# Splitting weights without GpSimd and adding taps in pairs ahead of TensorE, in a dynamic convolution with a gated MLP

## The chip, the cores and the metric

The kernel runs on one core of a Trainium2 chip. The metric is the device time of one launch in microseconds (us). The kernel before was timed three times: 1320.76, 1321.1 and 1321.77 us, median 1321.1 us.

## The reference

Two steps follow each other. For each of 4 x 4096 positions a softmax over 7 taps (8 heads) weighs the position and the six before it; then each of the 16384 rows of 192 goes through a gated MLP of width 1536.

```python
w = softmax(weight_gen)                     # over the last axis, 7 taps, per head
out = einsum('bshk,bskhg->bshg', w, x_unf)  # x_unf: the row and the six rows before it
g, val = out @ w_gate, out @ w_val          # 192 -> 1536, twice
y = (g * sigmoid(g) * val) @ w_out          # 1536 -> 192
```

x and weight_gen are fp32; the three weight matrices arrive as float64, two 32-bit words per number.

## The kernel before, in words

**Groups and steps.** The 16384 rows are 32 groups (g) of 512 rows: 128 partitions by JG = 4. The width of 1536 is 12 blocks (f) of 128. A step (g, f) makes the two products of one block for one group (lines L464 to L487, 18 matmuls of 512 columns), ScalarE's silu (L491), VectorE's product h (L500 for groups 0 and 1, L505 for the others), and, two steps later, the product with w_out (L539 or L550 and L559). PSUM has four banks for `up`, which is two steps: step s+2 can't begin before VectorE has read the sums of step s. An fp32 operand is split into a high part and a low rest (`hi` by a copy on ScalarE, `lo` by a subtraction), and three products are added.

**Order of the steps** (L645 to L649). Steps 0 to 3 are (0, 0) to (0, 3); then (1, f) and (0, f + 4) alternate up to step 19; (1, 8) to (1, 11) are steps 20 to 23, and from step 24 on the groups come one after the other. Nothing reorders instructions: each engine runs them in the order in which this Python emits them. A dictionary `todo` holds, by step, the pieces of other work that are emitted around h of that step. In steps 0 to 3 all pieces come ahead of h, later only the first one.

**Blocks of weights** (`weight_ops`, L387 to L450). Each block of 128 columns becomes fp32 and is split. In the kernel before a block takes five DMAs on SP's queue (L380), the exponent's bits (L394, VectorE), Relu and Sign (L403, L405, ScalarE), sign times scale (L406, GpSimd), the mantissa in two operations (L411, L421, VectorE), the value (L434, VectorE), copies on ScalarE (L384, L448) and two subtractions on GpSimd (L385). Later `wo32` is split too (L384, L385, called at L663).

**The first two groups** (`summed_turn`, L274 to L299). Each of the seven taps is a product x times weight on VectorE (L230), a copy of 64 columns on ScalarE (L286), and eight transposing matmuls against an identity, added up in PSUM (L289). The tile `xatt` has two buffers. From group 2 on VectorE adds the taps itself (L230, L251) and the turn goes by a 32x32 transpose and DMAs (L304 to L342). `split_ops` (L344 to L363) splits the turned sums.

**GpSimd's queue.** TensorE's sum of one step is made by two half-arrays. `told` (L265) puts a nop on GpSimd's queue that waits for the first part of the sum; `behind` makes the first matmul of the second part (L483) wait for that nop. So the nop also waits for all that stands ahead of it on GpSimd's queue.

Of the kernel before, what the change touches and what calls it, by code (L numbers as in the profile page):

```python
# [18 lines left out]
def dynconv_glu_kernel(  # L19
# [23 lines left out]
    nc = tc.nc  # L43
# [41 lines left out]
    ident = const.tile([P, P], F32, name="ident")  # L85
    warm = const.tile([P, 1], F32, name="warm")
    exp_bias = const.tile([P, 1], F32, name="exp_bias")
    wa_hi = const.tile([P, 2, F], F32R, name="wa_hi")
    wa_lo = const.tile([P, 2, F], F32R, name="wa_lo")
    wb_hi = const.tile([P, F], F32R, name="wb_hi")  # L90
    wb_lo = const.tile([P, F], F32R, name="wb_lo")
    wo = const.tile([P, NF, 2, D], F32R, name="wo")
    wo32 = const.tile([P, NF, D], F32, name="wo32")

# [126 lines left out]
    def attention_ops(g):  # L221
        cx, cw = chunk_of(xcuts, g), chunk_of(wcuts, g)
        jx, jw = g * JG - xcuts[cx][0], g * JG - wcuts[cw][0]
        last = K - 1
        tmp = {}

        def mul(engine, k, into):
            src = x_t[cx][:, jx + k : jx + k + JG].rearrange("p t (h i) -> p t h i", h=H)
            w = e_t[cw][:, jw : jw + JG, :, k : k + 1].to_broadcast([P, JG, H, G])
            engine.tensor_tensor(  # L230
                out=into.rearrange("p t (h i) -> p t h i", h=H), in0=src, in1=w, op=ALU.mult
            )

        if g < MOVED:
            return mul

        def first():
            xatt[g] = att.tile([P, JG, 2 * P], F32, tag="xatt", name="xatt")
# [35 lines left out]
    def summed_turn(g):  # L274

        mul = attention_ops(g)
        if g == 0:
            ps = [ps_up.tile([P, NC], F32, tag="up", name="tr") for _ in range(2)]
        else:
            ps = [ps_dn.tile([P, NC], F32, tag=f"dn{2 + n}", name=f"tr{n}") for n in range(2)]  # L280

        def tap(k):
            def go():
                a = att.tile([P, JG, 2 * P], F32, tag="xatt", name="xatt")
                mul(nc.vector, k, a[:, :, 0:D])
                nc.scalar.activation(out=a[:, :, D:], in_=a[:, :, P:D], func=AF.Copy)  # L286
                for half in range(2):
# [16 lines left out]
    def turn_ops(g):  # L304

        whole = {}

        def blocks():
            cut = att.tile([P, JG, D], F32, tag="cut", name="cut", bufs=1)
            cut = whole["cut"] = cut.rearrange("p t d -> p (t d)").rearrange(  # L310
                "p (i t c) -> p i t c", i=NB, t=JG
            )
            nc.vector.transpose(
                cut, xatt[g][:, :, 0:D].rearrange("p t (i r) -> p i t r", i=NB)
            )
# [27 lines left out]

    def split_ops(g, ps):  # L344
# [15 lines left out]

            return go

        return [high(0), low(0), high(1), low(1)] if g < MOVED else [high(1), low(1), high(0), low(0)]  # L363


    NW = 3 * P + D
    raw_t = {}

    def load_weights(f):
        raw = stage.tile([P, NW, 2], I32, tag="raw", name="raw", bufs=RAW)  # L370
        fs = slice(f * P, (f + 1) * P)
        pieces = (
# [4 lines left out]
            (raw[:, 3 * P : NW], w_out[fs]),  # L377
        )
        for dst, src in pieces:
            nc.sync.dma_start(out=dst.rearrange("p n w -> p (n w)"), in_=src.bitcast(I32))  # L380
        raw_t[f] = raw

    def split(hi, lo, src):
        nc.scalar.activation(out=hi, in_=src, func=AF.Copy)  # L384
        nc.gpsimd.tensor_tensor(out=lo, in0=src, in1=hi.bitcast(F32), op=ALU.subtract)  # L385

    def weight_ops(f):  # L387
        st = {}
# [2 lines left out]
        def exponent():  # L391
# [28 lines left out]
        def mantissa_low():  # L420
# [5 lines left out]
                op0=ALU.logical_shift_right,  # L426
                op1=ALU.bitwise_or,
            )
            if f + RAW < NF:
                load_weights(f + RAW)  # L430

        def value32():
            w = stage.tile([P, NW], F32, tag="w", name="w")
            nc.vector.scalar_tensor_tensor(  # L434
                out=w,
                in0=st["m"],
                scalar=float(2**24),
                in1=st["scale"],
                op0=ALU.add,
                op1=ALU.mult,  # L440
            )
            split(wb_hi[:, fs], wb_lo[:, fs], w[:, 2 * P : 3 * P])
            split(
                wa_hi[:, :, fs],
                wa_lo[:, :, fs],
                w[:, 0 : 2 * P].rearrange("p (i n) -> p i n", i=2),
            )
# [164 lines left out]
    with tc.manual_schedule():  # L612
        nc.gpsimd.memset(exp_bias, -920.0 * TWO23)

        nc.scalar.activation(out=warm, in_=exp_bias, func=AF.Exp)
        now, soon = load_x(0)
        for op in load_taps(0) + [now]:
            op()
        load_weights(0)
        load_weights(1)  # L620
        soon()
        for f in range(2, RAW):
# [9 lines left out]
        for op in after[:6]:  # L632
            op()
        ps, taps = summed_turn(0)
        meanwhile = w0 + w1[:2]
        for op in taps[:2] + after[6:]:
            op()
        for op, other in zip(meanwhile, taps[2:] + [lambda: None]):
            op()
            other()  # L640
# [13 lines left out]
        for f in range(2, NF):  # L654
# [31 lines left out]
        for i in range(len(steps) + LAG + 1):  # L686
# [67 lines left out]
```

## Time and profile before

| | |
|---|---|
| median of three runs | 1321.1 us |
| the profiled execution's own time | 1320.99 us |
| its span | 1319.2 us |
| TensorE busy | 1284.0 us (97%) |
| VectorE busy | 1006.8 us (76%) |
| ScalarE busy | 589.6 us (45%) |
| GpSimd busy | 49.9 us (4%) |
| mean granted TensorE clock | 0.990 |
| TensorE's chain L483, L471, L550, L474 | 22%, 22%, 19%, 18% of the span |

A row of a view of groups or of the timeline gives the line of the kernel, the engine, the operation, what is written from what, the shape, and how many; a timeline row begins with the start and the duration in us, and in brackets stands the idle time ahead of it and what ended it. A busy share near 100% on TensorE says that matmuls follow each other, not that the array is at its peak. The whole execution has few idle places; the view by slices shows them in the first two or three of forty slices and in the last.

### The profile page before, as it was taken

Reading aid. Unit: us, or ns where it says so; the run is one execution under the profiler, and the core shown is the slowest. Engines: PE = TensorE matmul, PEld = TensorE weight load, DVE = VectorE, ACT = ScalarE, POOL = GpSimd, SP = SyncE. Lnnn points to the kernel's source line nnn. Section 1 sums busy time; section 2 is a strip of 40 time slices with the busy share of each in tenths; the row PEclk is TensorE's granted clock in tenths of the full one; section 3 lists DMA queues with packets and bytes.
Section 4 is the critical chain, followed back from the end, with each engine's and each line's share of the span. In section 5 each row is a group of like instructions: output and inputs, shape, how many; then the busy total and the mean of one; then the engine's idle time right before and its main releaser. Section 6 shows DMA issues by size and latency. Waiting matters only on the chain.

```text
span 1319.2 us, 31481 instructions
## 1 busy us (share of the span) xinstructions
PE 1284.0 (97%) x13280; PEld 1233.0 (93%) x13280; DVE 1006.8 (76%) x1397; ACT 589.6 (45%) x1039; POOL 49.9 (4%) x59
## 2 busy tenths in 40 slices
PE   6898999999999999999999999999999999999997
PEld 5777888889999999999999999999999999999997
DVE  7368787778887777888777798777778877777843
ACT  4235344454444345444444544444454444444443
POOL 4234000000000000000000000000000000000000
PEclk9899999999999999999999999999999999999999
DMA  6230221211122121122212112221211212111010
GB/s 178 72 124 13 62 83 30 83 42 47 54 57 75 38 83 41 26 71 62 71 42 83 38 27 73 59 71 42 82 29 31 80 31 81 41 42 34 20 42 13
DMA packets 64150, 74.89 MB, mean 57 GB/s; under 512 B 6924, under 2 KB 53516, under 8 KB 62216
## 3 DMA queue, kind: packets, MB, share of 16 engines
q1 hardware_dynamic: 64008, 72.89, 20.1%
q8 instruction: 103, 1.69, 0.5%
q14 instruction: 39, 0.32, 0.1%
HBM read 48.48 MB, written 24.38 MB: 55 GB/s over the span
## 4 chain that ended last, share of the span: by engine, by line
PE 89%; DVE 5%; ACT 3%; issue 2%; DMA 1%; POOL 0%; SPq 0%; ACTq 0%; DVEq 0%; POOLq 0%
PE up L483 22%; PE up L471 22%; PE dn L550 19%; PE up L474 18%; PE dn L559 3%; PE tr L289 2%; PE dn L539 1%; DVE h L505 1%; DVE prod L230 1%; ACT sg L491 1%; DVE lo L508 0%; DVE xatt L230 0%; ACT L491 0%; ACT L183 0%; DVE m L421 0%
## 5 line engine op out<-in xcount | busy, mean ns | idle before, releaser
L550 PE MATMUL dn<-wo,hi 64*128 64x384 f32 x2880 | 553.9, 344 | 0.4 <-ACT hi L506 0.4
L559 PE MATMUL dn<-wo,lo 64*128 64x192 f32 x2880 | 487.8, 249 | 0.3 <-DVE lo L508 0.3
L550 PEld LDWEIGHTS dn<-wo,hi 64*128 64x128 f32 x2880 | 449.2, 184 | 11.0 <-ACT osb L588 1.4
L559 PEld LDWEIGHTS dn<-wo,lo 64*128 64x128 f32 x2880 | 428.6, 186 | 4.5 <-DVE lo L508 0.5
L506 ACT ACTIVATE hi<-h 128x512 fp32r<-128x512 f32 x360 | 228.3, 634 | 359.1 <-DVE h L505 359.1
L505 DVE TENSOR_TENSOR h<-up,sg 128x512 f32<-128x512 f32 x360 | 248.0, 689 | 179.4 <-ACT sg L491 179.2
L491 ACT ACTIVATE sg<-up 128x512 f32<-128x512 f32 x384 | 228.9, 596 | 339.3 <-PE up L483 330.4
L508 DVE TENSOR_TENSOR lo<-h,hi 128x512 fp32r<-128x512 f32 x360 | 246.6, 685 | 80.4 <-ACT hi L506 80.4
L483 PE MATMUL up<-xhi,wa_hi 64*128 64x512 f32 x768 | 214.7, 421 | 8.3 <-POOLq L267 8.1
L471 PE MATMUL up<-xhi,wb_hi 64*128 64x512 f32 x768 | 216.0, 421 | 5.0 <-ACT xhi L349 4.1
L471 PE MATMUL up<-xlo,wb_hi 64*128 64x512 f32 x768 | 203.9, 392 | 1.6 <-DVE xlo L356 1.5
L471 PE MATMUL up<-xhi,wb_lo 64*128 64x512 f32 x768 | 204.7, 394 | 0.0
L474 PE MATMUL up<-xhi,wa_hi 64*128 64x512 f32 x768 | 203.4, 391 | 0.0
L474 PE MATMUL up<-xhi,wa_lo 64*128 64x512 f32 x768 | 203.4, 391 | 0.0
L483 PE MATMUL up<-xhi,wa_lo 64*128 64x512 f32 x768 | 202.8, 390 | 0.0
L474 PE MATMUL up<-xlo,wa_hi 64*128 64x512 f32 x768 | 202.4, 388 | 0.0
L483 PE MATMUL up<-xlo,wa_hi 64*128 64x512 f32 x768 | 202.0, 388 | 0.0
L251 DVE TENSOR_TENSOR xatt<-xatt,prod 128x768 f32<-128x768 f32 x180 | 172.5, 958 | 0.0
L230 DVE TENSOR_TENSOR prod<-xt,wt 128x768 f32<-128x768 f32 x180 | 171.5, 953 | 0.2
L483 PEld LDWEIGHTS up<-xhi,wa_hi 64*128 64x128 f32 x768 | 121.8, 185 | 11.7 <-POOLq L267 11.6
L471 PEld LDWEIGHTS up<-xhi,wb_hi 64*128 64x128 f32 x768 | 121.7, 184 | 7.6 <-ACT xhi L349 4.6
L474 PEld LDWEIGHTS up<-xhi,wa_hi 64*128 64x128 f32 x768 | 122.0, 185 | 5.6
(56 smaller groups left out, 1326.8 us busy)
## 6 DMA issues: line engine op xcount, KB each, us to landing
xt<-in_x_dram SPq DMA_DIRECT2D x14, 1344.0 KB, 6.9
turned<-cut SPq DMA_DIRECT2D x120, 96.0 KB, 2.0
out_dram<-osb SPq DMA_DIRECT2D x116, 96.0 KB, 1.9
t<-turned SPq DMA_DIRECT2D x60, 128.0 KB, 2.6
t<-turned SPq DMA_DIRECT2D x30, 256.0 KB, 2.9
raw<-in_moe_w_out_dram SPq DMA_DIRECT2D x12, 192.0 KB, 2.7
wt<-in_weight_gen_dram SPq DMA_DIRECT2D x3, 672.0 KB, 5.6
raw<-in_moe_w_gate_dram SPq DMA_DIRECT2D x12, 128.0 KB, 2.3
```

The costliest lines, as they stand in the source:

```text
L230: engine.tensor_tensor(out=into.rearrange("p t (h i) -> p t h i", h=H), in0=src, in1=w, op=ALU.mult)
L251: nc.vector.tensor_tensor(out=a, in0=a, in1=tmp.pop(k), op=ALU.add)
L289: nc.tensor.matmul(ps[half][:, t * P : (t + 1) * P], a[:, t, half * P : (half + 1) * P], ident, start=(k == 0 and t == 0), stop=(k == K - ...
L471: nc.tensor.matmul(ps, w[r, fs], m[r], start=(n == 0), stop=False)
L474: ins = nc.tensor.matmul(sums[i], w[r, i, fs], m[r], start=False, stop=False)
L483: ins = nc.tensor.matmul(sums[i], w[r, i, fs], m[r], start=False, stop=(n == len(full) - 1))
L491: nc.scalar.activation(out=sg, in_=sums[0], func=AF.Silu)
L505: nc.vector.tensor_tensor(out=h, in0=sums[1], in1=sg, op=ALU.mult)
L506: nc.scalar.activation(out=hi, in_=h, func=AF.Copy)
L508: nc.vector.tensor_tensor(out=lo, in0=h, in1=hi.bitcast(F32), op=ALU.subtract)
L550: nc.tensor.matmul(acc[g, t], hi[r, cs], wo[r, f].rearrange("p a d -> p (a d)"), start=opens, stop=False,)
L559: nc.tensor.matmul(acc[g, t][:, 0:D], lo[r, cs], wo[r, f, 0], start=False, stop=closes)
```

## The change

- `SUMS`: group 0's taps go to TensorE as five tiles (0), (1), (2), (3+4), (5+6), group 1's as four, (0+1), (2+3), (4+5), (6). VectorE makes the products and adds a pair; `xatt` has three buffers. A turn starts with its upper half, which needs ScalarE's copy.
- In group 1 the products of tile n stand in the order before step n (those of tile 0 before step 0), and its turn behind the matmuls of step n.
- No work but nops and memsets is left on GpSimd: the sign is put into the scale's bits by one VectorE operation (`value32`), the Sign on ScalarE is gone, and the rests of a block are one subtraction on VectorE (`low32`, 128x384). The high parts of a block are one copy on ScalarE. The rest of `wo` is VectorE's too.
- Block 0's five DMAs are issued from ScalarE's queue, first of all, in place of SP's queue behind x.
- The order around the first steps is written anew; the third piece of the first softmax (`after[6:]`) moves from ahead of the third tap to step 5.

```diff
+    SUMS = {0: ((0,), (1,), (2,), (3, 4), (5, 6)), 1: ((0, 1), (2, 3), (4, 5), (6,))}
...
-    wa_hi = const.tile([P, 2, F], F32R, name="wa_hi")
...
+    w_hi = const.tile([P, 3, F], F32R, name="w_hi")
+    w_lo = const.tile([P, 3, F], F32R, name="w_lo")
+    wa_hi, wa_lo, wb_hi, wb_lo = w_hi[:, 0:2], w_lo[:, 0:2], w_hi[:, 2], w_lo[:, 2]
...
+            def product(k, first):
+                def go():
+                    if first:
+                        a["sum"] = att.tile([P, JG, 2 * P], F32, tag="xatt", name="xatt", bufs=3)
+                        mul(nc.vector, k, a["sum"][:, :, 0:D])
+                    else:
+                        a["other"] = att.tile([P, JG, D], F32, tag="prod", name="prod")
+                        mul(nc.vector, k, a["other"])
...
+            def add():
+                x = a["sum"][:, :, 0:D]
+                nc.vector.tensor_tensor(out=x, in0=x, in1=a.pop("other"), op=ALU.add)
+            def twice():
+                x = a["sum"]
+                nc.scalar.activation(out=x[:, :, D:], in_=x[:, :, P:D], func=AF.Copy)
+            def turn():
+                for half in (1, 0):
                     for t in range(JG):
                         nc.tensor.matmul(
...
-        return [high(0), low(0), high(1), low(1)] if g < MOVED else [high(1), low(1), high(0), low(0)]
+        return [high(1), low(1), high(0), low(0)]
...
     def split(hi, lo, src):
         nc.scalar.activation(out=hi, in_=src, func=AF.Copy)
-        nc.gpsimd.tensor_tensor(out=lo, in0=src, in1=hi.bitcast(F32), op=ALU.subtract)
+        nc.vector.tensor_tensor(out=lo, in0=src, in1=hi.bitcast(F32), op=ALU.subtract)
...
-            nc.scalar.activation(out=sign, in_=raw[:, :, 1], func=AF.Sign)
-            nc.gpsimd.tensor_tensor(out=sign, in0=sign, in1=e.bitcast(F32), op=ALU.mult)
...
+        def value32():
+            scale = st["e"]
+            nc.vector.scalar_tensor_tensor(
+                out=scale, in0=st["raw"][:, :, 1], scalar=-(2**31), in1=scale,
+                op0=ALU.bitwise_and, op1=ALU.bitwise_or,
+            )
...
+            st["w"] = w[:, 0 : 3 * P].rearrange("p (i n) -> p i n", i=3)
+            nc.scalar.activation(out=w_hi[:, :, fs], in_=st["w"], func=AF.Copy)
             nc.scalar.activation(out=wo32[:, f], in_=w[:, 3 * P : NW], func=AF.Copy)
+        def low32():
+            nc.vector.tensor_tensor(
+                out=w_lo[:, :, fs], in0=st["w"], in1=w_hi[:, :, fs].bitcast(F32), op=ALU.subtract,
+            )
+        return [exponent, mantissa_high, mantissa_low, value32, low32]
...
+        load_weights(0, nc.scalar)
         nc.scalar.activation(out=warm, in_=exp_bias, func=AF.Exp)
...
-        load_weights(0)
...
-        meanwhile = w0 + w1[:2]
-        for op in taps[:2] + after[6:]:
...
-        for op in turns[0::2] + w1[2:4] + turns[1:2] + w2[:1] + turns[3:]:
+        for op in (
+            tap(0) + w0[0:1] + tap(1) + w0[1:2] + tap(2) + w0[2:4] + tap(3) + w0[4:5]
+            + tap(4) + w1[0:3] + turns[0:2] + w1[3:4] + turns[2:4] + w1[4:5] + w2[0:2]
+        ):
...
-        todo[0] = [w2[1], w3[0], w2[2]]
         ps1, taps1 = summed_turn(1)
+        for op in taps1[0][0]:
+            op()
+        turns = {n: turn for n, (_, turn) in enumerate(taps1)}
+        todo[0] = [w2[2], w3[0], w2[3], w3[1], w2[4], w3[2]]
+        for n in range(1, HEAD):
+            todo.setdefault(n - 1, []).extend(taps1[n][0])
...
-            for part, ahead in ((3, 2), (1, 3), (0, 4), (2, 3)):
-                if (f, part) not in ((2, 1), (2, 2), (2, 0), (3, 0)):
+            for part, ahead in ((3, 2), (0, 4), (1, 3), (2, 3), (4, 2)):
+                if f > 3 or part > 2:
                     todo.setdefault(max(due[f] - ahead, 0), []).append(convert[f][part])
-        spread(taps1, 0, HEAD - 1)
-        spread(split_ops(1, ps1), HEAD - 1, HEAD)
+        todo[HEAD - 1] += split_ops(1, ps1)
         spread(load_x(1) + load_taps(1), LOAD1, LOAD1 + 7)
+        spread(after[6:], HEAD + 1, HEAD + 2)
...
+            if i in turns:
+                turns[i]()
```

## Rows read from the trace of the kernel before

**Rows 1.** Windows by stage; columns: us, busy of PE, PEld, DVE, ACT, POOL, PEclk, DMA

```profile
0.00:24.73 24.73, 14.65 (x114) 14.30 (x114) 19.28 (x31) 11.73 (x22) 10.32 (x15) 1.00 0.65 189
24.73:64.28 39.55, 31.22 (x213) 26.08 (x214) 17.80 (x27) 14.02 (x33) 10.31 (x12) 0.82 0.30 90
64.28:70.93 6.65, 6.61 (x35) 5.35 (x36) 1.74 (x4) 0.01 (x1) 0.52 (x1) 0.51 0.01 2
70.93:131.65 60.72, 52.61 (x515) 44.88 (x512) 50.12 (x63) 29.64 (x61) 27.57 (x30) 1.00 0.24 74
131.65:200.00 68.35, 68.35 (x716) 60.28 (x714) 54.87 (x75) 28.47 (x51) 1.21 (x2) 1.00 0.24 71
```

**Rows 2.** Waits of PE from 0 to 140 us: total, times, longest

```profile
PE tr L289 <- DVE xatt L230: 10.6, 2, 9.4
PE up L483 <- POOLq L267: 8.1, 7, 1.6
PE up L471 <- ACT xhi L349: 4.1, 2, 3.4
```

**Rows 3.** Timeline of PE: where steps 20 and 21 begin

```profile
131.65 0.53 PE L471 MATMUL up<-xhi,wb_hi 64*128 64x512 f32 x2
...
135.02 0.52 PE L471 MATMUL up<-xhi,wb_hi 64*128 64x512 f32 x2
```

**Rows 4.** Timeline: L411 and L421 on VectorE with GpSimd idle, L411 beside GpSimd

```profile
30.09 0.45 DVE L411 TENSOR_SCALAR m<-raw 128x576 int32<-128x576 int32 x1
30.58 0.76 DVE L421 SCALAR_TENSOR_TENSOR m<-raw,m 128x576 int32<-128x576 int32 x1
...
119.02 1.82 POOL L406 TENSOR_TENSOR sign<-sign,e 128x576 f32<-128x576 f32 x1 [1.05 <-ACT sign L405]
...
119.48 1.68 DVE L411 TENSOR_SCALAR m<-raw 128x576 int32<-128x576 int32 x1
```

**Rows 5.** Timeline of VectorE: instructions that follow each other without idle time

```profile
106.06 0.94 DVE L230 TENSOR_TENSOR prod<-xt,wt 128x768 f32<-128x768 f32 x1
106.93 0.74 DVE L434 SCALAR_TENSOR_TENSOR w<-m,sign 128x576 f32<-128x576 int32 x1
107.60 0.68 DVE L500 TENSOR_TENSOR hi<-up,sg 128x512 f32<-128x512 f32 x1
108.20 0.67 DVE L394 TENSOR_SCALAR e<-raw 128x576 int32<-128x576 int32 x1
...
113.16 0.74 DVE L421 SCALAR_TENSOR_TENSOR m<-raw,m 128x576 int32<-128x576 int32 x1
113.82 0.84 DVE L170 TENSOR_REDUCE mx<-wt 128x96 f32<-128x672 f32 x1
```

**Rows 6.** Timeline of VectorE at the start: two lengths of one operation, with GpSimd idle

```profile
4.55 0.62 DVE L177 TENSOR_TENSOR wt<-wt,mx 128x448 f32<-128x448 f32 x1
...
6.19 0.39 DVE L200 TENSOR_TENSOR wt<-wt,sm 128x224 f32<-128x224 f32 x1
```

**Rows 7.** Groups of ScalarE by form, 0 to 150 us: copies of two lengths

```profile
L384 ACT ACTIVATE wa_hi<-w 128x256 fp32r<-128x256 f32 x12 | 4.9, 405 | 0.0
...
L384 ACT ACTIVATE wb_hi<-w 128x128 fp32r<-128x128 f32 x12 | 3.7, 309 | 3.4 <-DVE w L434 3.4
```

**Rows 8.** Timeline at the start: the pads' DMAs, the first taps, group 0's turns

```profile
2.12 3.77 SPq L152 DMA_DIRECT2D xt<-in_x_dram  x8
...
8.29 1.83 DVE L230 TENSOR_TENSOR xatt<-xt,wt 128x768 f32<-128x768 f32 x2 [0.19 <-DMA raw<-in_moe_w_val_dram]
...
9.39 14.64 PE L289 MATMUL tr<-ident,xatt 128*128 128x128 f32 x112 [9.39 <-DVE xatt L230]
```

**Rows 9.** Window of the first 5 us (columns as in rows 1)

```profile
0.00:5.00 5.00, 0.00 (x0) 0.00 (x0) 1.85 (x4) 1.88 (x3) 4.36 (x9) 1.00 0.64 195
```

**Rows 10.** Timeline of ScalarE around the softmax of the second chunk, in step 16

```profile
118.89 1.28 ACT L183 ACT_TABLE_LOAD   x1
120.19 1.33 ACT L183 ACTIVATE wt<-wt 128x1344 f32<-128x1344 f32 x1
121.53 1.28 ACT L491 ACT_TABLE_LOAD   x1
122.83 0.60 ACT L491 ACTIVATE sg<-up 128x512 f32<-128x512 f32 x1
```

More of the change, by code (lines that the diff above doesn't have):

```diff
@@ L87, in dynconv_glu_kernel @@
     exp_bias = const.tile([P, 1], F32, name="exp_bias")
-    wa_hi = const.tile([P, 2, F], F32R, name="wa_hi")
-    wa_lo = const.tile([P, 2, F], F32R, name="wa_lo")
-    wb_hi = const.tile([P, F], F32R, name="wb_hi")
-    wb_lo = const.tile([P, F], F32R, name="wb_lo")
+    w_hi = const.tile([P, 3, F], F32R, name="w_hi")
+    w_lo = const.tile([P, 3, F], F32R, name="w_lo")
+    wa_hi, wa_lo, wb_hi, wb_lo = w_hi[:, 0:2], w_lo[:, 0:2], w_hi[:, 2], w_lo[:, 2]
     wo = const.tile([P, NF, 2, D], F32R, name="wo")
@@ L237, in first @@
         def first():
-            xatt[g] = att.tile([P, JG, 2 * P], F32, tag="xatt", name="xatt")
+            xatt[g] = att.tile([P, JG, 2 * P], F32, tag="xatt", name="xatt", bufs=3)
             mul(nc.vector, 0, xatt[g][:, :, 0:D])
@@ L280, in summed_turn, with tap @@
             ps = [ps_dn.tile([P, NC], F32, tag=f"dn{2 + n}", name=f"tr{n}") for n in range(2)]
[L282 to L287, printed above, removed]
+        parts = SUMS[g]
+        def tap(n):
+            a = {}
+            def product(k, first):
[6 more added lines that the diff above has]
+                        mul(nc.vector, k, a["other"])
+                return go
+            def add():
[6 more added lines that the diff above has]
+                for half in (1, 0):
                     for t in range(JG):
@@ L290, in go @@
                             ps[half][:, t * P : (t + 1) * P],
-                            a[:, t, half * P : (half + 1) * P],
+                            a["sum"][:, t, half * P : (half + 1) * P],
                             ident,
-                            start=(k == 0 and t == 0),
-                            stop=(k == K - 1 and t == JG - 1),
-                        )
-            return go
-        return ps, [tap(k) for k in range(K)]
+                            start=(n == 0 and t == 0),
+                            stop=(n == len(parts) - 1 and t == JG - 1),
+                        )
+            made = [product(k, m == 0) for m, k in enumerate(parts[n])]
+            return made + [add] * (len(made) - 1) + [twice], turn
+        return ps, [tap(n) for n in range(len(parts))]
     Q = 32
@@ L317, in places @@
         def places():
-            t32 = att.tile([P, JG, 2 * P], F32, tag="xatt", name="t32")
+            t32 = att.tile([P, JG, 2 * P], F32, tag="xatt", name="t32", bufs=3)
             t32 = whole["t32"] = t32.rearrange("p t d -> p (t d)").rearrange(
@@ L361, in low, with load_weights @@
             return go
-        return [high(0), low(0), high(1), low(1)] if g < MOVED else [high(1), low(1), high(0), low(0)]
+        return [high(1), low(1), high(0), low(0)]
     NW = 3 * P + D
     raw_t = {}
-    def load_weights(f):
+    def load_weights(f, queue=nc.sync):
         raw = stage.tile([P, NW, 2], I32, tag="raw", name="raw", bufs=RAW)
@@ L379, in load_weights @@
         for dst, src in pieces:
-            nc.sync.dma_start(out=dst.rearrange("p n w -> p (n w)"), in_=src.bitcast(I32))
+            queue.dma_start(out=dst.rearrange("p n w -> p (n w)"), in_=src.bitcast(I32))
         raw_t[f] = raw
@@ L403, in exponent @@
             nc.scalar.activation(out=e, in_=e, func=AF.Relu, scale=TWO23, bias=exp_bias)
-            sign = stage.tile([P, NW], F32, tag="sign", name="sign")
-            nc.scalar.activation(out=sign, in_=raw[:, :, 1], func=AF.Sign)
-            nc.gpsimd.tensor_tensor(out=sign, in0=sign, in1=e.bitcast(F32), op=ALU.mult)
-            st["scale"] = sign
+            st["e"] = e
         def mantissa_high():
@@ L428, in mantissa_low @@
             )
+        def value32():
+            scale = st["e"]
+            nc.vector.scalar_tensor_tensor(
+                out=scale,
+                in0=st["raw"][:, :, 1],
+                scalar=-(2**31),
+                in1=scale,
+                op0=ALU.bitwise_and,
+                op1=ALU.bitwise_or,
+            )
             if f + RAW < NF:
                 load_weights(f + RAW)
-        def value32():
             w = stage.tile([P, NW], F32, tag="w", name="w")
@@ L437, in value32 @@
                 scalar=float(2**24),
-                in1=st["scale"],
+                in1=scale.bitcast(F32),
                 op0=ALU.add,
@@ L441, in value32 @@
             )
[L442 to L446, printed above, removed]
-            )
-            nc.scalar.activation(out=wo32[:, f], in_=w[:, 3 * P : NW], func=AF.Copy)
-        return [exponent, mantissa_high, mantissa_low, value32]
+            st["w"] = w[:, 0 : 3 * P].rearrange("p (i n) -> p i n", i=3)
+            nc.scalar.activation(out=w_hi[:, :, fs], in_=st["w"], func=AF.Copy)
+            nc.scalar.activation(out=wo32[:, f], in_=w[:, 3 * P : NW], func=AF.Copy)
+        def low32():
+            nc.vector.tensor_tensor(
+                out=w_lo[:, :, fs],
+                in0=st["w"],
+                in1=w_hi[:, :, fs].bitcast(F32),
+                op=ALU.subtract,
+            )
+        return [exponent, mantissa_high, mantissa_low, value32, low32]
     h_t = {}
@@ L634, in dynconv_glu_kernel, with tap @@
         ps, taps = summed_turn(0)
-        meanwhile = w0 + w1[:2]
-        for op in taps[:2] + after[6:]:
[L637 to L640, printed above, removed]
+        def tap(n):
+            made, turn = taps[n]
+            return made + [turn]
         turns = split_ops(0, ps)
-        for op in turns[0::2] + w1[2:4] + turns[1:2] + w2[:1] + turns[3:]:
+        for op in (
+            tap(0) + w0[0:1] + tap(1) + w0[1:2] + tap(2) + w0[2:4] + tap(3) + w0[4:5]
+            + tap(4) + w1[0:3] + turns[0:2] + w1[3:4] + turns[2:4] + w1[4:5] + w2[0:2]
+        ):
             op()
@@ L649, in dynconv_glu_kernel @@
         steps += [(g, f) for g in range(2, NG) for f in range(NF)]
-        todo[0] = [w2[1], w3[0], w2[2]]
         ps1, taps1 = summed_turn(1)
+        for op in taps1[0][0]:
[4 more added lines that the diff above has]
+            todo.setdefault(n - 1, []).extend(taps1[n][0])
         due = [steps.index((0, f)) for f in range(NF)]
-        for f in range(2, NF):
-            for part, ahead in ((3, 2), (1, 3), (0, 4), (2, 3)):
-                if (f, part) not in ((2, 1), (2, 2), (2, 0), (3, 0)):
+        for f in range(3, NF):
+            for part, ahead in ((3, 2), (0, 4), (1, 3), (2, 3), (4, 2)):
+                if f > 3 or part > 2:
                     todo.setdefault(max(due[f] - ahead, 0), []).append(convert[f][part])
-        spread(taps1, 0, HEAD - 1)
-        spread(split_ops(1, ps1), HEAD - 1, HEAD)
+        todo[HEAD - 1] += split_ops(1, ps1)
         spread(load_x(1) + load_taps(1), LOAD1, LOAD1 + 7)
+        spread(after[6:], HEAD + 1, HEAD + 2)
         for f in range(NF):
```

## The prediction, made before the changed kernel was run

> **What bounds the kernel now.** I read the windows by stage first [rows 1]. From 131.65 us on, TensorE is busy for all of 68.35 us; that is the start of step 20, and up to the tail the trace looks like this, so what is saved ahead of it is saved at the end, and nothing else is. Ahead of it stand four stages: the turns of group 0 up to the first product (24.73 us), steps 0 to 3 with group 1's turns (39.55), step 4 (6.65), and steps 5 to 19 (60.72). A step of the undisturbed stretch takes 135.02 - 131.65 = 3.37 us [rows 3], so sixteen steps are worth 53.9 us where steps 4 to 19 take 67.4. The waits of TensorE come next [rows 2]: 9.4 us are the start, 8.1 us in 7 pieces are waits at L483 for GpSimd's queue, 4.1 us wait for a turned group's high part. The nop of L267 has no work; it is late because L406 and L385 stand ahead of it. Third is the granted clock: 0.51 in step 4, where 3.37 us of work take 6.65 at 1.2 GHz after a long wait, and 0.82 in the second stage [rows 1]. Last I looked at VectorE beside GpSimd: L411 takes 0.45 us alone and 1.68 us beside L406 [rows 4].
>
> **Prices.** VectorE's instructions overlap a little, so I count from start to start [rows 5]: product or addition 0.87, L434 0.67, h 0.60, L421 0.66. L394 and L411 are 0.45 alone [rows 4], 0.37 where the next is independent. The new sign operation has the form of L421: 0.66, with 0.08 more where the next needs it. `low32` has no row. By length, 0.62 us for 448 and 0.39 for 224 columns [rows 6] make 0.55 us for 384, 0.47 from start to start; the rests of `wo` (192) make 0.36 and 0.28. Bounds are the 224 and the 448 row. ScalarE's copy of 384 columns is 0.51 by 0.309 for 128 and 0.405 for 256 [rows 7]. A block on VectorE is then 0.37 + 0.45 + 0.66 + 0.74 + 0.67 + 0.47 = 3.4 us, three old operations at their price without GpSimd, plus 1.2 new.
>
> **Block 0 from ScalarE's queue.** It frees SP's queue of five issues, and the first Exp comes later by those five issues on ScalarE; the softmax then ends some 0.2 us later. Against it: its 590 KB now move beside x and the eight pads, whose issue lasts until 5.89 us [rows 8]. In 0 to 5 us the DMA engines are 0.64 busy at 195 GB/s [rows 9], so full they give about 305 GB/s (an estimate) and 590 KB are 1.9 us of them. The delay of the first tap lies between 0 and 1.9 us (a gain is excluded: that tap waits for x, not for block 0, and VectorE's softmax is ready only 0.19 us earlier [rows 8]); 0.36 x 5 = 1.8 us are free in that window, so I take 0.5. The Trainium skill ("DMA: Bandwidth & Descriptors", section "Issuing engines are not separate DMA queues") says that another issuing engine only saves issue time, since all run on the same DMA engines; by that alone the whole 1.9 us would be paid, and the sum below would be 1303.4.
>
> **Group 0's turns.** Five turns replace seven, each 14.64 / 7 = 2.1 us [rows 8]; but now VectorE is ahead of them. From 8.29 us it has 7 products, 2 additions (7.8) and block 0 (3.4), with hand-overs 11.4, to 19.7; the copy ends at 20.2, the last turn at 22.3. The upper half's hi and lo are ready by 22.7. The lower half's copy stands on ScalarE behind block 1's copies, which wait for VectorE's two operations: hi at 25.5, lo at 26.25. So the first full step starts only about a microsecond earlier than now.
>
> **Steps 0 to 3.** `h` follows all other pieces there, so VectorE's list sets the pace. From 26.25 us: block 1's rest 0.5, blocks 2 to 4 10.2, one operation of block 5 0.4, seven products and three additions 8.7, three h 1.9: 21.7 us. Waits that I walked through add 4.1: the copy ahead of each `low32`, dependent neighbours, and in step 3 ScalarE's silu, block 4's copies and Relu ahead of group 1's hi. Step 4 starts at 51.95, with the 0.5 of the DMAs 52.45, where it is 64.28 now: **11.8 us saved**. Four turns at 2.1 us and four steps lie beside this list; if TensorE runs them at 1.2 GHz, up to 7 us of this are given back (a turn is then about 2.6 us, a step twice 3.37).
>
> **Step 4.** TensorE's wait ahead of it shrinks from the 3.4 us that stand in [rows 2] to about 1.2 (a turn ends at 50.8), so I take full clock and 3.5 us: **3.15 saved**; at 0.51 nothing.
>
> **Steps 5 to 19.** At 3.37 us these are 50.6 us. VectorE has per pair of steps a block 3.4, two h 1.2, two operations of group 2's taps 1.74, a rest of `wo` 0.28: 6.6 of 6.74 us. On top come the moved softmax piece and one more product in step 5 (2.1), five more rests of `wo` in step 10 (1.4), and four softmax operations in steps 12 to 15 (3.1). VectorE falls behind, and step s+2 waits for h(s). Walking through it, TensorE waits 0.1, 0.65, 0.2 and 1.2 us at steps 13, 15, 16 and 17. In step 16 ScalarE has two table loads and an Exp ahead of silu, 3.9 us [rows 10], which now start later, behind VectorE's subtraction: 3.5 us at step 18, then 0.45. Sum 6.1, the stage 56.7 in place of 60.72: **4.0 saved**. The waits for GpSimd's queue are gone, and two thirds of their gain goes into waits for VectorE.
>
> **Sum.** 11.8 + 3.15 + 4.0 = 18.95 us. The profiled execution took 1320.99 us, the median of the runs is 1321.1, the same. 1321.0 - 18.95 = 1302.0 us. The three buffers, the later order of a split from group 2 on (unchanged there) and SP's shorter queue cost nothing: TensorE is without idle time there [rows 1].
>
> **Rivals.** (a) *TensorE stays the bound in steps 5 to 19.* Only about 1.1 of the 6.1 us of waits remains, if VectorE is some 5% faster than my walk; VectorE was busy 50.12 of 60.72 us with GpSimd's interference in it [rows 1], which speaks for it; 41 more VectorE operations speak against it. 1297. (b) *VectorE's instructions don't overlap.* With the durations in place of start to start some 90 instructions in steps 4 to 19 cost 0.08 us more each, 7.2 us, all on the path: 1309. Against it, the next starts 0.07 to 0.08 us before the end of the last in [rows 5]; for it, dependent neighbours do not overlap. The Trainium skill ("VectorE: DVE Perf Modes", section "The DRAIN you can't avoid") says that the next operation does not start until the pipeline is empty, which is this case; the trace disagrees with it for independent neighbours. (c) *The nops stay late though GpSimd is empty*, so that the change doesn't do what it says: 8.1 us are kept, 1310. Against it, TensorE has no wait in 68.35 us with the same nops [rows 1]. (d) *Slower: the long durations are VectorE's own and not GpSimd's doing.* The place is steps 0 to 17: 12 sign operations, 12 `low32`, 12 rests of `wo` and 5 additions are 12 x (0.66 + 0.47 + 0.28) + 5 x 0.87 = 21.3 us of new work, nearly all on the path. Once they cost 1.9 times my prices the saving is gone; at L411's 1.68 to 0.45 it is far past that, at twice the price 1323. Against it, every long L411 that I saw stands beside a GpSimd instruction [rows 4].
>
> **How the numbers follow.** Forecast 0.60, (a) 0.15, (b) 0.17, (c) 0.05, (d) 0.03. A measurement can tell about 0.2% (2.6 us) from no change. Faster by more: all but (d) and a sliver of the others, 0.95; same 0.02; slower 0.03. The range reaches from (a) without the DMAs' 0.5, 1296.5, to (b), 1309.5; the low clock in steps 1 to 4 and the DMAs' other end lie in it, and (c), (d) are left out.
>
> **What would show it.** Right: no wait at L483 for GpSimd's queue; L411 at 0.45 throughout; step 4 beginning near 52 us at a clock near 1; waits at L471 for h in steps 13 to 18, the longest behind the Exp; step 20 near 113 us. Wrong: a clock of 0.5 in step 4, a first tap at 9 us or later, VectorE idle for h in every step (then (a)), or step 20 at a later place than 119 us, which only (b) or (c) would bring.

## The result, and the profile after

The changed kernel takes 1306.03 us, median of four runs (1305.64 to 1307.03), against 1320.93 us for the kernel before: ratio 0.9888, 95% interval 0.987 to 0.9905, 14.9 us less. The forecast was 1302.0 us, with a range of 1296.5 to 1309.5. The profiled execution took 1305.82 us, its span is 1304.0 us. Lines have moved: the products L471, L474, L483 are now L502, L505, L514; h is L531, silu L522, the turn L309; L394, L411, L421, L434 are L415, L429, L439, L461; new are the sign L450, the copy of a block's high parts L470 and its rest L474.

Windows by stage, cut at the first product, at steps 4, 5 and 20, and 68.35 us further (columns as in [rows 1]):

```profile
0.00:24.66 24.66, 11.11 (x81) 10.64 (x82) 17.60 (x31) 8.68 (x16) 4.95 (x11) 1.00 0.64 189
24.66:54.52 29.86, 24.60 (x166) 18.90 (x166) 24.52 (x38) 10.95 (x23) 0.00 (x0) 0.83 0.38 112
54.52:58.37 3.85, 3.63 (x34) 2.95 (x36) 2.23 (x4) 0.43 (x1) 0.00 (x0) 1.00 0.34 113
58.37:116.45 58.08, 53.03 (x514) 45.49 (x513) 52.73 (x90) 24.70 (x48) 0.00 (x0) 1.00 0.23 71
116.45:184.80 68.35, 68.35 (x716) 61.57 (x715) 55.91 (x78) 28.39 (x51) 0.00 (x0) 1.00 0.24 72
```

Beside [rows 1]: the first stage is no shorter, steps 0 to 3 take 29.86 us in place of 39.55, step 4 3.85 in place of 6.65 at full clock, steps 5 to 19 58.08 in place of 60.72. Step 20 starts at 116.45 in place of 131.65 us, 15.2 us earlier, and from there TensorE is again without idle time. VectorE is busy 24.52 of 29.86 us in steps 0 to 3, where it was 17.80 of 39.55, and 52.73 of 58.08 us in steps 5 to 19.

Waits of PE from 0 to 130 us (total, times, longest), to be held against [rows 2]:

```profile
PE tr L309 <- ACT xatt L304: 15.1, 4, 12.2
PE up L502 <- ACT sg L522: 2.5, 1, 2.5
PE up L502 <- ACT w_hi L470: 2.3, 4, 0.9
PE up L505 <- ACT xhi L370: 2.0, 1, 2.0
PE up L502 <- ACT xhi L370: 1.1, 1, 1.1
```

No wait for GpSimd's queue is left. The start has grown from 9.4 to 12.2 us. The rows at L502 are the places where TensorE runs into VectorE and ScalarE. The start, on SP's queue and on VectorE (timeline):

```profile
3.59 4.96 SPq L152 DMA_DIRECT2D xt<-in_x_dram  x8
...
10.60 0.96 DVE L230 TENSOR_TENSOR xatt<-xt,wt 128x768 f32<-128x768 f32 x1 [1.48 <-DMA raw<-in_moe_w_gate_dram]
```

The eight pads (the DMAs that fetch the six rows ahead of each partition's first row of x) are issued from 3.59 to 8.55 us, not from 2.12 to 5.89, and the first tap starts at 10.60, not at 8.29 [rows 8]. The bracket names a load of weights, which the tap doesn't read; it reads x, whose last pad is issued at 8.24 us. SP's queue itself waits 3.3 us between the pads, for DMAs of block 0 (waits of SP, 0 to 14 us); before, it waited 0.3 us there:

```profile
SPq L152 <- DMA raw<-in_moe_w_gate_dram: 2.4, 2, 1.5
SPq L152 <- DMA raw<-in_moe_w_val_dram: 0.7, 1, 0.7
...
SPq L152 <- DMA raw<-in_moe_w_out_dram: 0.2, 1, 0.2
```

And steps 7 and 8, as a sample of how VectorE and ScalarE share the stretch (timeline):

```profile
71.03 0.68 DVE L531 TENSOR_TENSOR hi<-up,sg 128x512 f32<-128x512 f32 x1
71.15 0.53 ACT L470 ACTIVATE w_hi<-w 128x384 fp32r<-128x384 f32 x1 [2.00 <-DVE w L461]
71.70 0.56 DVE L474 TENSOR_TENSOR w_lo<-w,w_hi 128x384 fp32r<-128x384 f32 x1
72.18 0.45 DVE L415 TENSOR_SCALAR e<-raw 128x576 int32<-128x576 int32 x1
72.55 0.95 DVE L251 TENSOR_TENSOR xatt<-xatt,prod 128x768 f32<-128x768 f32 x1
72.67 0.78 ACT L424 ACTIVATE e<-e,exp_bias 128x576 int32<-128x576 int32 x1 [0.74 <-DVE e L415]
73.35 0.58 ACT L522 ACTIVATE sg<-up 128x512 f32<-128x512 f32 x1
73.42 0.46 DVE L429 TENSOR_SCALAR m<-raw 128x576 int32<-128x576 int32 x1
73.96 0.69 DVE L531 TENSOR_TENSOR hi<-up,sg 128x512 f32<-128x512 f32 x1
```

ScalarE's Relu (L424) waits for VectorE's exponent, and silu (L522), which h needs, stands behind the Relu.

The changed kernel was run once more with the last experiments:

> The changed kernel once more, beside these: 1306 by both theories; first tap within 0.7 us of 10.60 and the distance from step 5 to step 20 within 0.2 us of 58.08.

It took 1306.62 us, first tap 10.61, steps 5 to 20 116.54 - 58.45 = 58.09 us. So the marks of these two traces agree to a tenth of a microsecond. The landing of the first DMAs scatters more: in the eight traces in which all of block 0 is issued first from ScalarE's queue, the first tap starts between 10.12 and 11.26 us; in the four in which it goes behind the pads on SP's queue, between 8.55 and 8.85.

### The profile page after: what moved, and what is told of

The parts are those of the page before. It is cut to its first block, busy times and chain, and to the rows that moved or that the text cites. A ratio compares the mean times of both kernels' runs of the same rounds, so it can differ in the third digit from the quotient of the medians.

```text
span 1304.0 us, 31222 instructions
## 1 busy us (share of the span) xinstructions
PE 1271.4 (97%) x13200; PEld 1226.0 (94%) x13200; DVE 1015.6 (78%) x1438; ACT 577.6 (44%) x1010; POOL 4.9 (0%) x11
## 3 DMA queue, kind: packets, MB, share of 16 engines
q8 instruction: 103, 1.69, 0.5%
## 4 chain that ended last, share of the span: by engine, by line
PE 86%; DVE 8%; ACT 3%; DMA 2%; issue 1%; SPq 0%; ACTq 0%; DVEq 0%
PE up L502 22%; PE up L514 22%; PE dn L581 20%; PE up L505 18%; PE dn L590 3%; DVE prod L230 1%; DVE h L536 1%; PE dn L570 1%; DVE xatt L230 1%; DVE hi L531 1%; ACT sg L522 1%; DVE e L450 1%; DVE m L439 1%; DVE w L461 1%; ACT L522 0%
## 5 line engine op out<-in xcount | busy, mean ns | idle before, releaser
L522 ACT ACTIVATE sg<-up 128x512 f32<-128x512 f32 x384 | 228.3, 594 | 305.5 <-PE up L514 296.8
L502 PE MATMUL up<-xhi,w_hi 64*128 64x512 f32 x768 | 214.9, 420 | 7.1 <-ACT sg L522 2.5
L514 PE MATMUL up<-xhi,w_hi 64*128 64x512 f32 x768 | 213.3, 421 | 0.2
L505 PE MATMUL up<-xhi,w_hi 64*128 64x512 f32 x768 | 202.0, 391 | 2.0 <-ACT xhi L370 2.0
L502 PE MATMUL up<-xhi,w_lo 64*128 64x512 f32 x768 | 203.7, 395 | 0.0
L502 PE MATMUL up<-xlo,w_hi 64*128 64x512 f32 x768 | 202.6, 391 | 0.3 <-DVE xlo L377 0.2
L505 PE MATMUL up<-xhi,w_lo 64*128 64x512 f32 x768 | 201.9, 391 | 0.0
L514 PE MATMUL up<-xhi,w_lo 64*128 64x512 f32 x768 | 201.3, 390 | 0.0
L505 PE MATMUL up<-xlo,w_hi 64*128 64x512 f32 x768 | 201.1, 388 | 0.2 <-DVE xlo L377 0.2
L514 PE MATMUL up<-xlo,w_hi 64*128 64x512 f32 x768 | 200.5, 387 | 0.0
L230 DVE TENSOR_TENSOR prod<-xt,wt 128x768 f32<-128x768 f32 x185 | 175.7, 950 | 0.2
L502 PEld LDWEIGHTS up<-xhi,w_hi 64*128 64x128 f32 x768 | 120.7, 184 | 11.3 <-ACT w_hi L470 3.5
L505 PEld LDWEIGHTS up<-xhi,w_hi 64*128 64x128 f32 x768 | 120.7, 185 | 6.8 <-ACT xhi L370 2.5
L505 PEld LDWEIGHTS up<-xlo,w_hi 64*128 64x128 f32 x768 | 120.9, 185 | 4.7 <-DVE xlo L377 0.5
```

What stands on the lines that cost most here:

```text
L230: engine.tensor_tensor(out=into.rearrange("p t (h i) -> p t h i", h=H), in0=src, in1=w, op=ALU.mult)
L502: nc.tensor.matmul(ps, w[r, fs], m[r], start=(n == 0), stop=False)
L505: ins = nc.tensor.matmul(sums[i], w[r, i, fs], m[r], start=False, stop=False)
L514: ins = nc.tensor.matmul(sums[i], w[r, i, fs], m[r], start=False, stop=(n == len(full) - 1))
L522: nc.scalar.activation(out=sg, in_=sums[0], func=AF.Silu)
```

## The experiments

**The start: where block 0 is issued.**

```diff
-        load_weights(0, nc.scalar)
         nc.scalar.activation(out=warm, in_=exp_bias, func=AF.Exp)
...
+        load_weights(0)
         load_weights(1)
```

Run `sp_queue`:

> Block 0's five DMAs go back to SP's queue behind x; all else as in the changed kernel. My theory (the pads' issue waits for block 0's landings): the first tap is back at about 8.3 us in place of 10.60, but VectorE then waits for block 0's exponent until about 11.2, so the second tap starts near 11.6 in place of 11.85 and step 20 at 116.2 in place of 116.45; time within 0.5 us of the changed kernel's 1306. Rival (the early block 0 is worth its queue): step 20 near 118.5 and 1308. Second rival (the head does not count, since VectorE's later backlog hides it): first tap at 8.3, step 20 unchanged to 0.1 us.

VectorE's timeline:

```profile
8.57 0.96 DVE L230 TENSOR_TENSOR xatt<-xt,wt 128x768 f32<-128x768 f32 x1 [0.48 <-DMA raw<-in_moe_w_gate_dram]
11.39 0.46 DVE L415 TENSOR_SCALAR e<-raw 128x576 int32<-128x576 int32 x1 [1.87 <-DMA raw<-in_moe_w_out_dram]
11.77 0.95 DVE L230 TENSOR_TENSOR xatt<-xt,wt 128x768 f32<-128x768 f32 x1
```

1305.6 us, step 20 at 116.34. The first tap is 2.0 us earlier, the second 0.08: what x gains, block 0 loses. So ScalarE's queue, by itself, is worth nothing in this order. Next, the same with the first operations of block 0 moved out of the way:

```diff
-            tap(0) + w0[0:1] + tap(1) + w0[1:2] + tap(2) + w0[2:4] + tap(3) + w0[4:5]
+            tap(0) + tap(1) + tap(2) + w0[0:4] + tap(3) + w0[4:5]
```

Run `sp_queue_late`:

> As sp_queue, and block 0's first two VectorE operations stand behind the third tap, so that nothing waits for its landing. My theory: first tap 8.3, no wait of VectorE for block 0, the whole chain on VectorE 2.0 to 2.3 us earlier, step 4 at 52.3 in place of 54.52, step 20 near 114.3 and about 1304. Rival (what follows hides the head): step 20 at 116.4, 1306.

1304.14 us, first tap 8.55, step 4 at 52.49, 2.0 us earlier than in the changed kernel; the distance from step 4 to step 18 is 53.90 us in both. So the 2 us at the start go through whole as far as step 18. Behind it 0.4 us are lost: step 20 is at 114.83 us, 1.6 us earlier. Both kernels wait 2.5 us ahead of step 18; after it the granted clock stays at 1.00 in the changed kernel and is 0.50 here (windows from the start of step 18, first the changed kernel, then this one):

```profile
108.42:111.40 2.98, 2.75 (x24) 2.25 (x26) 2.98 (x5) 0.69 (x2) 0.00 (x0) 1.00 0.02 5
```

```profile
106.39:109.42 3.03, 3.02 (x11) 2.10 (x13) 3.03 (x5) 0.69 (x2) 0.00 (x0) 0.50 0.02 5
```

TensorE gets 11 matmuls done where the other gets 24, and step 18 takes 1.69 us more than 3.37, there 1.18. In `turns_first` and `raw_two_early` below it is as here (clock 0.51 and 0.50, 1.74 and 1.69 us), in `sp_queue` as in the changed kernel (1.00, 1.18). Why the clock falls after this wait in some kernels and not in others, no run shows.

What holds the pads, I tried to tell apart:

```diff
+        load_weights(0, nc.scalar, slice(0, 2))
...
+        load_weights(0, part=slice(2, 5))
         load_weights(1)
```

Run `raw_two_early`:

> Only two of block 0's five DMAs (256 of 576 KB) are issued first from ScalarE's queue, the other three from SP's queue behind the pads; block 0's first VectorE operations stand behind the third tap. Theory A (the pads are late because their issue waits for the landing of block 0's DMAs): five pads now wait for early landings only, the first tap comes at 8.4 to 8.8 us, as with all of block 0 on SP's queue (8.55). Theory B (the pads share the DMA engines with block 0's bytes): 256 of 576 KB cost 0.45 of the 2.0 to 2.3 us, first tap at 9.3 to 9.5.

SP's queue and VectorE (timeline):

```profile
2.13 5.30 SPq L152 DMA_DIRECT2D xt<-in_x_dram  x8
...
9.66 2.69 DVE L230 TENSOR_TENSOR xatt<-xt,wt 128x768 f32<-128x768 f32 x3 [0.62 <-DMA raw<-in_moe_w_gate_dram]
```

9.66 us: outside both bounds, A's by 0.9 us and B's by 0.2. So theory A alone doesn't explain the delay; B is near. The pads start at 2.13 us again and still take until 7.43: SP's queue waits 1.3 us for x itself, which is 0.8 in `sp_queue_late`, and 0.6 for one of block 0's DMAs. 256 KB cost 9.66 - 8.55 = 1.1 us, 576 KB 10.60 - 8.55 = 2.05: more bytes cost more, but this is one trace with a start that scatters, and 44% of the bytes cost 54% of the delay. 1305.65 us.

**The order ahead of step 0.**

```diff
-            + tap(4) + w1[0:3] + turns[0:2] + w1[3:4] + turns[2:4] + w1[4:5] + w2[0:2]
+            + tap(4) + w1[0:3] + turns + w1[3:4] + w2[0:2] + w1[4:5]
```

Run `turns_first`:

> In the list ahead of step 0 the four splits of group 0's turned sums stand together, ahead of block 1's last two operations; all else as in the changed kernel. My theory (the lower half's copy waits on ScalarE behind block 1's copies and so behind VectorE): TensorE's wait of 2.0 us at the second line of the first product and VectorE's 1.3 us go, VectorE's list runs 1.0 to 1.3 us earlier, step 4 starts at 53.2 to 53.5 in place of 54.52, time near 1305. Rival (TensorE's waits ahead of step 4 are worth nothing, VectorE's order only shifts): step 4 at 54.5.

Step 4 at 52.98, 1.5 us earlier, a little more than expected; the 2.0 us wait at L505 is gone. But TensorE's wait ahead of the next turn grows from 1.6 to 4.1 us: what counts is that VectorE no longer waits 1.3 us for the lower half's copy. At step 20 (115.40) 1.05 us are left, since step 18 runs at the lower clock here. 1305.56 us against 1306.62 of the changed kernel beside it. So the lower half's copy behind block 1's copies was a loss that the new order had made.

**Where VectorE sets the pace.**

```diff
-            todo.setdefault(max(due[f] + 3, HEAD + 6), []).append(
+            todo.setdefault(max(due[f] + 3, 2 * NF - 4 + f // 4), []).append(
```

Run `wo_late`:

> The twelve splits of the output weights move from steps 10 to 22 to steps 20 to 22, where VectorE has time. My theory (VectorE's work sets steps 10 to 19): 10 subtractions of 0.28 us = 2.8 us leave VectorE's list ahead of step 20; the waits of 0.8, 0.4 and 0.9 us at steps 13, 15 and 17 shrink below 0.3 each, and the one at 18 by about 0.5; step 20 1.5 to 2.5 us earlier, near 114.5, time near 1304. Rival (TensorE or the Exp in ScalarE's queue is the bound there): less than 0.5 us.

The waits at L502 for the high parts fall from 2.3 us to this (waits of PE, 0 to 135 us):

```profile
PE up L502 <- ACT sg L522: 2.6, 1, 2.6
...
PE up L502 <- ACT w_hi L470: 0.7, 1, 0.7
```

1304.37 us; steps 5 to 19 take 114.41 - 57.64 = 56.77 us, 1.3 less. Step 20 is 2.0 us earlier, but 0.7 of that was there at step 5 already: the first tap came at 10.12. VectorE and ScalarE have less work ahead of step 20 (the splits' copies on ScalarE move too), and TensorE waits less, with its own work unchanged. The waits ahead of steps 13 and 15 are gone; ahead of 17 1.02 us are left, where I expected less than 0.3. The wait of 2.6 us behind the Exp stayed, and after it the granted clock fell (0.63 on average from 105.57 to 108.50 us), so that step 18 takes 2.08 us more than 3.37 in place of 1.18. That wait:

```diff
-    EXP1 = 16
+    EXP1 = 17
```

Run `exp_late`:

> The Exp of the second chunk one step later (17 in place of 16), the softmax operations ahead of it in their steps as they are, those behind it in step 19. My theory (the 2.5 us wait at step 18 is the Exp standing behind VectorE's late subtraction and ahead of silu): the Exp no longer waits for VectorE, the wait shrinks to about 1.1 us one step later, and step 21 starts about 1.5 us earlier than 119.82; time near 1304.5. Rival (two table loads and the Exp, 3.9 us, are the whole of it, wherever they stand): the same wait one step later, 1306.

ScalarE around the Exp, first in the changed kernel, then here (timelines; in both the Exp is the third line):

```profile
103.05 0.78 ACT L424 ACTIVATE e<-e,exp_bias 128x576 int32<-128x576 int32 x1 [0.74 <-DVE e L415]
103.84 1.28 ACT L183 ACT_TABLE_LOAD   x1
105.14 1.32 ACT L183 ACTIVATE wt<-wt 128x1344 f32<-128x1344 f32 x1
106.48 1.28 ACT L522 ACT_TABLE_LOAD   x1
107.78 0.60 ACT L522 ACTIVATE sg<-up 128x512 f32<-128x512 f32 x1
```

```profile
104.05 0.35 ACT L405 ACTIVATE wo<-wo 128x192 fp32r<-128x192 f32 x1
104.42 1.28 ACT L183 ACT_TABLE_LOAD   x1
105.71 1.33 ACT L183 ACTIVATE wt<-wt 128x1344 f32<-128x1344 f32 x1
107.06 1.28 ACT L522 ACT_TABLE_LOAD   x1
108.36 0.60 ACT L522 ACTIVATE sg<-up 128x512 f32<-128x512 f32 x1
```

1302.79 us, twice what I expected. Beside the 3.37 us of a step, steps 17, 18 and 19 take 2.94, 1.18 and 0.11 us more in the changed kernel (102.11, 108.42, 112.97, 116.45), and 0.12, 0.61 and 0.30 here (101.95, 105.44, 109.42, 113.09). The Exp takes the same time; in the changed kernel silu of step 16 stood behind it, after Relu and table load had waited for a late VectorE. One step later silu of step 16 goes first, and the table load starts right behind a copy on ScalarE instead of behind a Relu that waited 0.74 us for VectorE.

**The conversion's engine.** The subtractions alone, and then all of the conversion, back on GpSimd:

```diff
-        nc.vector.tensor_tensor(out=lo, in0=src, in1=hi.bitcast(F32), op=ALU.subtract)
+        nc.gpsimd.tensor_tensor(out=lo, in0=src, in1=hi.bitcast(F32), op=ALU.subtract)
...
-            nc.vector.tensor_tensor(
+            nc.gpsimd.tensor_tensor(
                 out=w_lo[:, :, fs],
```

Run `rests_gpsimd`:

> Only the subtractions (a block's rest and the rest of the output weights) go back to GpSimd; the sign stays on VectorE. My theory: VectorE loses 24 operations (12 x 0.47 + 12 x 0.28 = 9 us, 6 of them ahead of step 20 in the stretch where it is late), but the nops of the matmul sums stand behind GpSimd's subtractions again, and VectorE's two-input operations get long beside them; waits at the first matmul of the second half for GpSimd's queue come back with 2 to 5 us; 1305 to 1309. Rival (VectorE's load alone decides, GpSimd's queue was harmless): 4 us faster, 1302.

1306.82 us, steps 5 to 19 59.18 us, 1.1 more, though VectorE has 24 operations less. PE's waits of 0 to 135 us:

```profile
PE up L514 <- POOLq L267: 7.7, 7, 2.4
```

The waits for GpSimd's queue are back, more than I expected, in place of those for VectorE. The second kernel also gives the sign back:

```diff
+            nc.scalar.activation(out=sign, in_=raw[:, :, 1], func=AF.Sign)
+            nc.gpsimd.tensor_tensor(out=sign, in0=sign, in1=e.bitcast(F32), op=ALU.mult)
...
-            nc.vector.scalar_tensor_tensor(
-                out=scale,
```

Run `conversion_gpsimd`:

> The whole conversion as before the change: sign by Sign on ScalarE and a product on GpSimd, subtractions on GpSimd; pairs, order and queue as in the changed kernel. My theory (GpSimd's queue and its hold on VectorE were most of the loss in steps 5 to 19): the waits for GpSimd's queue come back with about 8 us and VectorE's L411 and L421 take up to 1.7 us beside it; 1311 to 1316, step 20 at 121 to 126. Rival (the pairs and the order made the gain, the engine of the conversion did not matter): within 1 us of 1306.

1314.16 us, steps 5 to 19 123.71 - 60.96 = 62.75 us. PE's waits of 0 to 135 us (L508 is L514 of the changed kernel, L432 below its L429):

```profile
PE up L508 <- POOLq L267: 13.1, 9, 1.9
```

VectorE's groups of the same stretch (at the end count, busy us, mean ns of one, idle time before), first in this kernel, then in the changed one:

```profile
L230 DVE TENSOR_TENSOR prod<-xt,wt 128x768 f32<-128x768 f32 x13 | 15.6, 1200 | 0.0
...
L432 DVE TENSOR_SCALAR m<-raw 128x576 int32<-128x576 int32 x12 | 9.9, 825 | 0.0
```

```profile
L230 DVE TENSOR_TENSOR prod<-xt,wt 128x768 f32<-128x768 f32 x15 | 14.3, 951 | 0.0
...
L429 DVE TENSOR_SCALAR m<-raw 128x576 int32<-128x576 int32 x12 | 5.4, 452 | 0.0
```

The products take 1200 ns beside GpSimd's work and 951 without, the mantissa 825 and 452. Both costs of GpSimd are real: the nops behind its instructions and VectorE's long instructions; no run separates them. The engine of the conversion is worth 8 to 9 of the 14.9 us: 1314.16 - 1306.03 = 8.1 across two sessions, or 14.9 - 5.6 = 9.3 with each against the kernel before in its own session (1319.76 - 1314.16 = 5.6).

**The pairs.** Seven turns for each group, four buffers, two turns behind a step:

```diff
-    SUMS = {0: ((0,), (1,), (2,), (3, 4), (5, 6)), 1: ((0, 1), (2, 3), (4, 5), (6,))}
+    SUMS = {g: ((0,), (1,), (2,), (3,), (4,), (5,), (6,)) for g in range(2)}
```

Run `no_pairs`:

> Both groups' taps go to TensorE one by one again (seven turns each, four buffers of the tile, two turns behind a step); conversion, order and queue as in the changed kernel. My theory (VectorE sets the pace up to step 4): VectorE has five additions less (4.4 us), TensorE five turns more (10.3 us at full clock, more at 1.2 GHz); in group 0 about 0 to 2 us are lost, in steps 0 to 3 3 to 5 us; step 4 at 57 to 61 in place of 54.52; time 1308 to 1312. Rival (the pairs bring nothing, VectorE gains by the lost additions what TensorE loses): 1306 or less.

Windows by stage, up to step 5:

```profile
0.00:28.25 28.25, 15.44 (x112) 15.35 (x112) 15.95 (x29) 9.52 (x18) 4.95 (x11) 1.00 0.58 165
28.25:61.05 32.80, 29.13 (x214) 23.79 (x214) 21.74 (x35) 11.97 (x26) 0.00 (x0) 0.90 0.41 115
61.05:64.90 3.85, 3.62 (x35) 2.95 (x36) 2.23 (x4) 0.43 (x1) 0.00 (x0) 1.00 0.02 4
```

1310.69 us. The first product is 3.6 us later (0.66 of it a first tap at 11.26), steps 0 to 3 take 2.9 us more, and TensorE is busy 29.13 of 32.80 us there, VectorE 21.74; in the last 7 us, from 54 to 61, they are busy 5.94 and 0.93. With seven turns TensorE, not VectorE, sets that pace. From step 5 to step 20 the two are alike, 58.08 us. The pairs are worth about 4 to 6 us.

**Together.**

Run `all_three`:

> sp_queue_late, wo_late and exp_late together. My theory: their savings lie in different stages and add up to 4.5 to 6.5 us against the changed kernel, 1299.5 to 1301.5, with step 20 near 111. Rival (each only uncovers the next wait): 1303 to 1304, no better than the best of them.

1299.48 us (1299.31 to 1299.86): the three add up, 6.5 us less than the changed kernel where the single gains make 6.8 (1.9, 1.7 and 3.2). Step 20 is at 109.05, 2 us earlier than I expected: without the wait behind the Exp step 18 takes only 0.36 us more than 3.37.

Run `four`:

> The three changes of all_three and the order of turns_first together. My theory: about 1 us less than all_three, 1298 to 1299, with step 4 near 51.5 and step 20 near 107.9. Rival (the head is hidden by what VectorE still has to do): 1299.5.

1298.08 us, ratio to the kernel before 0.9834, interval 0.982 to 0.9849; step 4 at 51.40, step 20 at 107.73. It beats both kernels. Its windows of steps 5 to 19 and of the time behind:

```profile
55.26:107.73 52.47, 51.79 (x514) 45.65 (x512) 49.58 (x78) 22.08 (x38) 0.00 (x0) 1.00 0.26 79
107.73:176.00 68.27, 67.86 (x703) 64.72 (x702) 57.73 (x88) 30.45 (x61) 0.00 (x0) 1.00 0.24 73
```

Steps 5 to 19 are now within 1.9 us of fifteen times 3.37 us; behind step 20 a part is given back. Steps 20 to 29 take 34.20 us (107.73 to 141.93), in the changed kernel 33.25 (116.45 to 149.70); 0.41 us of it is idle time of TensorE in the window shown. `wo_late` alone and `exp_late` alone don't lose this (33.25 each).

## Why the prediction was right, and where its terms were off

Direction and range held, and so did the main mechanism: GpSimd's waits go, VectorE sets the pace, and part of the gain goes into waits for it. Every term came out smaller than forecast. Of 18.95 us, 15.2 came in the trace: up to step 4 9.76 of 11.8, step 4 2.80 of 3.15, steps 5 to 19 2.64 of 4.0. One sign that the prediction had named for being wrong did come: a first tap at 9 us or later.

**Block 0 from ScalarE's queue** is the term that was most mis-sized: the first tap is 2.3 us later than before in place of the 0.5 that I took, and beyond the 1.9 that I gave as an end. Against `sp_queue`, where only the queue differs, it is 10.60 - 8.57 = 2.03 us, and 1.9 between the means of the eight traces and the four (10.59 and 8.66), so that end was about the price; taking 0.5 was the error. The share of free DMA time in the first window was taken as cover, but the pads are issued late: SP's queue waits 3.3 us between them for DMAs of block 0 to land. `sp_queue` is 0.1 us earlier at step 20 (116.34 against 116.45), no more than two traces of the changed kernel differ, so the queue as such is worth nothing. That another issuing engine saves only issue time is what the Trainium skill ("DMA: Bandwidth & Descriptors", section "Issuing engines are not separate DMA queues") states; this run agrees, with 2.03 us where I had put 1.9 beside it.

**Group 0's turns and steps 0 to 3**: with the start's 2.3 us taken off, group 0's lower lo ends at 26.35 (forecast 26.25) and step 4 starts at 52.2 (51.95; the walk's own terms, 26.25 + 21.7 + 4.1, make 52.05). The up to 7 us for the lower clock were not given back, though the granted clock was 0.50 from 30 to 38 us. `low32` takes 0.55 us, the sign 0.75, as priced; the heading of [rows 6], with GpSimd idle, does not hold for its first row, since a memset ran there from 2.94 to 5.08 us, but the price came out right. That VectorE's list sets this pace is shown by `sp_queue_late` and `turns_first`, which move step 4 by what they save; that it needs the pairs by `no_pairs`.

**Step 4** ran at full clock, as taken; 3.85 us in place of 3.5 came from hi and lo of group 1 coming one after the other.

**Steps 5 to 19**: waits of 7.5 us in place of 6.1, ahead of steps 13 (1.05), 15 (0.72), 17 (1.33), 18 (2.94) and 19 (1.18), where I had 0.1, 0.65, 1.2, 3.5 and 0.45; the 0.2 that I had at step 16 is 0.08. What I left out of the walk is ScalarE's order: in every second step silu stands behind the Relu, so that VectorE's L429 and h start 0.54 us apart in place of 0.37, and `low32` 0.67 behind h in place of 0.60, a quarter of a microsecond per pair of steps, 1 us by step 13. And the releaser of the waits ahead of steps 13, 15, 17 and 19, the steps that need a new block, is named as the copy of that block's high parts (L470); I had named h alone. For step 13, which begins at 86.40 us (timeline):

```profile
85.71 0.68 DVE L531 TENSOR_TENSOR hi<-up,sg 128x512 f32<-128x512 f32 x1
85.83 0.52 ACT L470 ACTIVATE w_hi<-w 128x384 fp32r<-128x384 f32 x1 [3.17 <-DVE w L461]
```

Copy and h end within 0.1 us of each other, so that no run tells which of them binds; both stand behind VectorE's L461, for which ScalarE waited 3.17 us. The wait ahead of step 18 is for silu behind the Exp. That these waits shrink when VectorE and ScalarE have less to do is shown by `wo_late`, and that the place of the Exp sets the one ahead of step 18 by `exp_late`.

**Rivals.** (a) didn't come: 58.1 us, not 52. `four` comes near it with 52.5, but only because VectorE's work was spread. (b) did not: start to start stayed at 0.87 us for products of 0.95 with an independent next. The section of the Trainium skill that the prediction set against its trace here ("VectorE: DVE Perf Modes", section "The DRAIN you can't avoid") goes on to say that a next operation that is not held starts earlier, so for independent neighbours the trace doesn't contradict it. (c) did not: no wait for GpSimd's queue. (d) did not: L429 was 0.45 us throughout, and long again in `conversion_gpsimd`.

**What stays open**: how much of the pads' delay is SP's waits for landings and how much slower landing itself; `raw_two_early` shows both, and more delay with more bytes, but not the shares. Open too are why the clock falls after the wait ahead of step 18 in some kernels only, and which of GpSimd's two costs is the larger.

## What to carry to other kernels

A handshake on an otherwise idle engine's queue is free only while that queue is empty: work put there later, for another reason, delays everyone who waits for the handshake (7.7 and 13.1 us here, with GpSimd's queue empty none). When work moves to an engine that is 80% busy, walk through its list step by step, with the in-order queue of the engine that it talks to, and then move what isn't due yet out of the crowded stretch; here that gave 1.7 us (`wo_late`) and 3.2 us (`exp_late`), and with the two repairs of the start 8 us in all. Loads that are issued first from another queue can still delay the loads that the first instruction waits for, here by about 2 us.

## What I had not expected of the hardware

At the lower clock level a turn in step 0 took 3.79 us (granted clock 0.50 between 32 and 38 us), against 2.05 at the full clock. I had put 2.6 from the kernel before, where three turns took 7.79 us from 32.26 us on; but the clock there rose from 0.50 to 1.00 on the way. 576 KB (the prediction's 590 KB are the same bytes, counted in thousands) issued ahead of x delayed the first tap by 2.0 us against `sp_queue`; at the 335 GB/s that the DMA engines moved between 3 and 5 us they are 1.8 us. And the same wait of 2.5 us ahead of step 18 is followed by a granted clock of 1.00 in the changed kernel and in `sp_queue`, and of 0.50 in `sp_queue_late` and `raw_two_early`.
